# Issuing the four loads of w_in in a different order among GpSimd's casts of v

## The chip, the cores and the metric

The kernel runs on one core of a Trainium2 chip. The metric is device time in microseconds (us) of one execution. Five engines run side by side, each with its own instruction list in a fixed order: PE (TensorE, matrix products), DVE (VectorE), ACT (ScalarE), POOL (GpSimd) and SP (SyncE). DMA transfers are issued by SP, ACT or POOL and are then carried out by the core's 16 DMA engines. An instruction that needs another engine's result waits on a semaphore, and everything behind it on its own engine waits with it.

## What is computed

The reference is sliding-window attention followed by a two-layer network:

```python
# q, k, v: (8 batches, 8 heads, 576 rows, 64)
scores = matmul(q, k^T) / 8;  keep 0 <= row - column < 64, else -1e9
attn   = softmax(scores);     x = matmul(attn, v)      # -> (4608 tokens, 512)
h      = x @ w_in                                       # w_in: (512, 2048)
g      = h / (1 + exp(-1.702 * h))
out    = g @ w_out                                      # w_out: (2048, 512)
```

Inputs and output are float32 in memory. The kernel computes in bf16 with float32 accumulation.

## The kernel before

The 4608 tokens are 36 tiles of 128, and four tiles make a chunk. For each tile the kernel forms the scores (`scores`, L325), the exponentials (`exp`, L340 and L342), the product with v (`pv`, L360), the division (`norm`, L376 and L378) and a transpose of x (`x_mm`, L426). For each chunk it then multiplies by w_in (`up_mm`, L464), applies the activation on ACT (`up_th`, L475) and DVE (`up_g`, L481), and multiplies by w_out (`down`, L494). The order of all instructions on all engines is written out by hand: a call in the source puts its instruction at the end of its engine's list. After L836 slots take over that order; the change touches only the start.

At the start the memory traffic is arranged so:

- **q and k of batch 0, first 512 rows.** SP issues four loads (`load_quads`, L125) and then two loads of v (`load_v(0, 0)`, `load_v(0, 2)`, L87). ACT issues `load_v(0, 1)` and `load_v(0, 3)` (L520, L521). v arrives as float32 in `stage_v`.
- **Casts of v.** `cast_v(b, i, parts=...)` (L101) turns a staged tile of v into bf16. Part 1 is the tile as it is (`v_nat`). Parts 0 and 2 are its two halves moved by 64 rows (`v_off`). `pv` needs both forms. The casts of tile 0 and part 1 of tile 3 are on DVE, the other casts of batch 0's tiles 1 to 3 on POOL. A cast on POOL waits for its tile's load, and what stands behind it on POOL waits too.
- **The weights.** `load_w_in(i)` (L242) is one DMA that POOL issues. It reads a quarter of w_in, casts it to bf16 on the way and writes `w_in_sb[i]`, 512 KB. `load_w_out(j)` (L248) does the same for a quarter of w_out. All eight go into POOL's one queue (q0), which the profile calls software_dynamic. `up_mm` of the first chunk works through w_in quarter by quarter (L580 on, L595 on, L616 on, L628 on).
- **Two gates.** At L522 POOL copies one element out of the last of the first loads, so that no weight is fetched before q and k have come. At L599 POOL copies one element of `w_in_sb[3]` into `stage_qk[0]`. SP's next loads begin with `load_pairs(0, 2)` (L169), which overwrites `stage_qk[0]`, so SP issues nothing from the second v load on until the last quarter of w_in has landed. Behind it SP issues `load_v(0, 4)`, `load_pairs(1, 0)`, two more v loads, and so on.
- **What follows the gate on POOL.** The casts of `load_pairs(0, 2)`, k then q (`cast_pair`, L113, called at L640 and L641), then `load_w_out(2)` and `load_w_out(3)` (L642, L643), then casts of v. On PE, after three groups of `down`, the cast pairs are transposed (`turn_mm`, L196, called at L662 and L663).

Of the kernel before, what the change touches and what calls it, by code (L numbers as in the profile page):

```python
# [29 lines left out]
def kernel(  # L30
# [39 lines left out]
    def size(i):  # L70
        return P if i < 4 else 64

    def heads(ap):
        return ap.rearrange("p (h d) -> p h d", d=D)
# [4 lines left out]
    def stage_of_v(b, i):  # L79
        return stage_v[5 if (b, i) == (0, 4) else i]  # L80
# [10 lines left out]
    def cast_v(b, i, engine=None, parts=(0, 1, 2)):  # L91
        n, vn, vo = size(i), v_nat[b % 2], v_off[b % 2]
        src = heads(stage_of_v(b, i)[:])
        pieces = [
            (vo[64:128, i, :, 0:D], src[0:64]),
            (vn[0:n, i, :, 0:D], src[0:n]),
            (vo[0:64, i + 1, :, 0:D], src[64:128]) if i < 4 else None,
        ]
        for p in parts:
            if pieces[p]:  # L100
                (engine or nc.gpsimd).tensor_copy(out=pieces[p][0], in_=pieces[p][1])  # L101
# [138 lines left out]
    def load_w_in(i):  # L240
        f = slice(512 * i, 512 * i + 512)
        nc.gpsimd.dma_start(  # L242
            out=w_in_sb[i][:], in_=moe_w_in.rearrange("(c p) f -> p c f", p=P)[:, :, f]
        )

    def load_w_out(j):
        f = slice(4 * j, 4 * j + 4)
        nc.gpsimd.dma_start(  # L248
            out=w_out_sb[:, f, :],
            in_=moe_w_out[512 * j : 512 * j + 512, :].rearrange("(p c) d -> p c d", c=4),  # L250
        )
# [269 lines left out]
    load_v(0, 3, nc.scalar)  # L521
    nc.gpsimd.tensor_copy(out=gate[0:1, 0:1], in_=stage_qk[1][0:1, 1, 0:1])  # L522
    load_w_in(0)
    cast_v(0, 1, parts=(0,))
    cast_v(0, 1, parts=(1,))
    cast_v(0, 1, parts=(2,))
    load_w_in(1)
    cast_v(0, 2, parts=(0,))
    cast_v(0, 2, parts=(1,))
    cast_v(0, 2, parts=(2,))  # L530
    cast_v(0, 3, parts=(0,))
    load_w_in(2)
    cast_v(0, 3, parts=(2,))
    load_w_in(3)
    load_w_out(0)
    load_w_out(1)
    cast_quads(0, 0, nc.vector)
# [490 lines left out]
```

## Time and profile before

| | us |
|---|---|
| median of 4 runs | 306.91 (306.19 to 308.47) |
| the profiled execution's own time | 306.75 |
| its span, first to last instruction | 305.0 |
| PE busy | 295.8 (97%) |
| DVE / ACT / POOL busy | 165.4 / 159.2 / 132.8 |
| share of 16 DMA engines: q0 (POOL's) / q1 / q10 (ACT's) | 66.7% / 46.3% / 3.7% |

A profile is one execution. Its time axis starts at the first instruction, and 1.75 us of the execution lie outside the span. In a timeline each line is one instruction or a run of equal ones: start, duration, engine, source line, what it writes and reads, and in square brackets how long the engine had been idle before it and what released it. "x128" is a count. Issue of a DMA and its landing are different things: the issue is an instruction on POOL, SP or ACT, and the landing comes us later, when the last of the 16 DMA engines has written its part. The DMA part of a profile gives bytes moved and the mean busy share of those engines in a stretch.

### The profile page before, as it was taken

What the parts mean: (1) busy time and instruction counts of PE and PEld (TensorE: products, weight loads), DVE (VectorE), ACT (ScalarE), POOL (GpSimd) and SP (SyncE); (2) the same over time, 40 slices, a digit from 0 to 9 for tenths busy, and PEclk for the clock granted to TensorE, in tenths of its full rate; (3) what the DMA queues carried; (4) which work ended last, traced back from release to release, by engine and by line L of the source; (5) the groups of instructions that cost most, each with busy time, mean ns of one, the idle gap of its engine ahead of it and who ended that gap; (6) DMA issues with size and microseconds to landing.
All of it is one profiled execution on the core that took longest, in us unless ns stands there. A gap on an engine that the chain in (4) does not pass through costs nothing.

```text
span 305.0 us, 8195 instructions
## 1 busy us (share of the span) xinstructions
PE 295.8 (97%) x3431; PEld 203.1 (67%) x3431; DVE 165.4 (54%) x286; ACT 159.2 (52%) x261; POOL 132.8 (44%) x191
## 2 busy tenths in 40 slices
PE   7799999999999999999999999999999999999995
PEld 6478454998666777777777777767776554444444
DVE  6467624797416364656647376475574754344300
ACT  3477434876436464755546465455565634444311
POOL 1380263853998679587685538573100000000000
PEclk9799999999999999999999999999999999999999
DMA  6989999998999999999999999999921202100121
GB/s 230 229 134 201 227 208 246 273 174 163 139 169 211 172 125 167 161 120 160 160 182 179 119 133 199 144 178 155 165 58 50 69 2 69 42 29 34 62 77 71
DMA packets 149621, 43.34 MB, mean 142 GB/s; under 512 B 135120, under 2 KB 144592, under 8 KB 149584
## 3 DMA queue, kind: packets, MB, share of 16 engines
q0 software_dynamic: 73008, 13.05, 66.7%
q1 hardware_dynamic: 72768, 26.23, 46.3%
q10 hardware_dynamic: 3808, 3.54, 3.7%
q8 instruction: 27, 0.44, 0.6%
q14 instruction: 10, 0.08, 0.1%
HBM read 36.70 MB, written 9.44 MB: 151 GB/s over the span
## 4 chain that ended last, share of the span: by engine, by line
PE 88%; DMA 6%; issue 3%; POOL 1%; ACT 1%; SPq 0%; DVE 0%; POOLq 0%
PE hps L464 39%; PE ops L494 37%; PE Tacc L360 4%; PE S L325 4%; DMA w_out_sb<-in_moe_w_out_dram 3%; DMA stage_qk<-in_k_dram 3%; PE ops L987 1%; PE S L317 1%; PE pxt L426 1%; SPq L125 0%; PE turn L196 0%; PE pxt L435 0%; POOL rows_q L113 0%; PE idle L515 0%; ACT PT L342 0%
## 5 line engine op out<-in xcount | busy, mean ns | idle before, releaser
L481 DVE SCALAR_TENSOR_TENSOR gT<-th,hps 128x512 bf16<-128x512 bf16 x144 | 98.3, 687 | 94.9 <-ACT th L475 94.9
L494 PE MATMUL ops<-w_out_sb,gT 128*128 128x512 bf16 x560 | 139.1, 379 | 0.3 <-DMA w_out_sb<-in_moe_w_out_dram 0.3
L464 PEld LDWEIGHTS <-w_in_sb 128*128 128x128 bf16 x1440 | 113.9, 113 | 31.0 <-issue 0.5
L475 ACT ACTIVATE th<-hps 128x512 bf16<-128x512 f32 x144 | 85.5, 598 | 87.9 <-PE hps L464 86.1
L494 PEld LDWEIGHTS <-gT 128*128 128x128 bf16 x560 | 52.1, 98 | 47.8 <-issue 0.6
L464 PE MATMUL hps<-xT_dma,w_in_sb 128*128 128x256 bf16 (+1 forms) x512 | 79.7, 299 | 0.0
L464 PE MATMUL hps<-xT_pe,w_in_sb 128*128 128x128 bf16 (+1 forms) x928 | 63.8, 225 | 0.0
L228 POOL COPY v_off<-v_nat 64x528 bf16<-64x528 bf16 x25 | 16.0, 639 | 38.6 <-DMA v_nat<-in_v_dram 36.4
L508 ACT ACTIVATE o_sb<-ops 128x512 f32<-128x512 f32 x33 | 19.8, 601 | 15.8 <-PE ops L494 15.8
L224 POOL DMA_DIRECT2D v_nat<-in_v_dram x25 | 21.5, 859 | 0.0
L223 POOL DMA_DIRECT2D rows_k<-in_k_dram x25 | 21.2, 850 | 0.0
L342 ACT ACTIVATE E<-S 128x1024 bf16<-128x1024 f32 x19 | 19.5, 1028 | 3.2 <-PE S L325 3.0
L223 POOL DMA_DIRECT2D rows_q<-in_q_dram x25 | 21.2, 847 | 0.0
L340 ACT ACTIVATE E<-S 128x512 bf16<-128x512 f32 x26 | 14.1, 594 | 12.6 <-PE S L325 12.6
L347 DVE TENSOR_TENSOR PT<-E,mask_None 128x1024 bf16<-128x1024 bf16 x25 | 17.9, 721 | 1.9 <-ACT E L342 1.7
L101 POOL CAST v_off<-stage_v 64x512 bf16<-64x512 f32 x24 | 15.5, 657 | 7.7 <-DMA stage_v<-in_v_dram 6.7
L403 DVE TENSOR_TENSOR xs<-Tacc,rc 128x896 bf16<-128x896 f32 (+1 forms) x26 | 18.0, 692 | 0.9
L360 PEld LDWEIGHTS <-PT 128*64 128x64 bf16 x576 | 11.0, 110 | 6.7 <-issue 5.9
L360 PE MATMUL Tacc<-v_off,PT 128*64 128x65 bf16 x320 | 13.5, 196 | 0.0
L230 POOL COPY v_off<-v_nat 64x528 bf16<-64x528 bf16 x20 | 12.9, 644 | 1.2
L325 PE MATMUL S<-qt,kt 64*128 64x64 bf16 x576 | 12.6, 192 | 0.0
L325 PEld LDWEIGHTS <-kt 64*128 64x128 bf16 x576 | 9.8, 96 | 4.1 <-issue 3.4
(74 smaller groups left out, 146.3 us busy)
## 6 DMA issues: line engine op xcount, KB each, us to landing
out_dram<-o_sb SPq DMA_DIRECT2D x24, 256.0 KB, 4.4
out_dram<-o_sb ACTq DMA_DIRECT2D x11, 256.0 KB, 2.0
stage_v<-in_v_dram SPq DMA_DIRECT2D x10, 256.0 KB, 5.7
rows_q<-in_q_dram POOLq DMA_DIRECT2D x20, 128.0 KB, 5.3
rows_k<-in_k_dram POOLq DMA_DIRECT2D x20, 128.0 KB, 6.3
v_nat<-in_v_dram POOLq DMA_DIRECT2D x20, 128.0 KB, 6.6
stage_qk<-in_q_dram SPq DMA_DIRECT2D x4, 512.0 KB, 6.7
stage_qk<-in_k_dram SPq DMA_DIRECT2D x4, 512.0 KB, 8.0
```

Of the source, the lines that this page charges most:

```text
L223: nc.gpsimd.dma_start(out=heads(rows[b % 2][w][0:n, i, :]), in_=rows_of(src, b, i))
L224: nc.gpsimd.dma_start(out=v_nat[b % 2][0:n, i, :, 0:D], in_=rows_of(v, b, i))
L325: nc.tensor.matmul(st[h % 2][:, t * 256 + hp * 64 : t * 256 + hp * 64 + 64], lhsT=src[1][part, hp, 64 * j : 64 * j + 128], rhs=src[0][part ...
L342: nc.scalar.activation(out=e[:], in_=st[:], func=AF.Exp, scale=scale)
L347: nc.vector.tensor_tensor(out=pt[:].rearrange("p a f -> p (a f)"), in0=E_of.pop(m)[:].rearrange("p a f -> p (a f)"), in1=masks[z][:].rearr ...
L360: nc.tensor.matmul(out_of(h)[t * 64 : t * 64 + 64, 0 : D + 1], lhsT=pt[:, epos : epos + 64], rhs=win, start=True, stop=True,)
L403: nc.vector.tensor_tensor(out=out[:, :, hs], in0=src[:, :, :, 0:D], in1=rc[:, :, hs].to_broadcast([P, 2, n, D]), op=ALU.mult,)
L464: nc.tensor.matmul(ps[:, g, :], lhsT=w_in[:, c, (f + g) % 4 : 512 : 4], rhs=xT[ch][:, m0 : m0 + nt // P, c, :], start=(c == 0), stop=(c == 3),
L475: nc.scalar.activation(out=th[:], in_=ps[:], func=AF.Tanh, scale=0.851)
L481: nc.vector.scalar_tensor_tensor(out=gT[ch, f // 4][:, f % 4 : f % 4 + nf, t0 : t0 + nt], in0=th[:], scalar=1.0, in1=ps[:], op0=ALU.add, o ...
L494: nc.tensor.matmul(O_of[ch, tsub][:, :], lhsT=gT[ch, j][:, f, tsub * P : (tsub + 1) * P], rhs=w_out_sb[:, 4 * j + f, :], start=(j == 0 and ...
L508: nc.scalar.activation(out=o_sb[:], in_=ps[:], func=AF.Copy, scale=0.5)
```

## The change

```diff
     load_w_in(0)
+    load_w_in(1)
+    load_w_in(2)
     cast_v(0, 1, parts=(0,))
     cast_v(0, 1, parts=(1,))
     cast_v(0, 1, parts=(2,))
-    load_w_in(1)
+    load_w_in(3)
     cast_v(0, 2, parts=(0,))
     cast_v(0, 2, parts=(1,))
     cast_v(0, 2, parts=(2,))
     cast_v(0, 3, parts=(0,))
-    load_w_in(2)
     cast_v(0, 3, parts=(2,))
-    load_w_in(3)
     load_w_out(0)
     load_w_out(1)
```

The lists of PE, DVE, ACT and SP are the same in both programs. On POOL the same instructions stand in another order: quarters 1 and 2 of w_in move ahead of the casts of v's tile 1, quarter 3 takes the place that quarter 1 had, and the remaining casts and the two loads of w_out follow without a load of w_in between them.

## The prediction

> **What bounds the kernel now.** I read the page first: PE is busy 97% of the span, and from slice 3 to the last but one every slice of PE shows 9. So a change at the start pays only as far as it removes PE's idle time. Next I read PE's waits between 20 and 60 us, by whom PE waited for; there are two:
>
> ```profile
> PE turn L196 <- POOL rows_q L113: 1.1, 1, 1.1
> PE ops L494 <- DMA w_out_sb<-in_moe_w_out_dram: 0.3, 1, 0.3
> ```
>
> PE's waits over the whole span add four before 12 us and none after 60 us. So no more than 1.09 + 0.31 = 1.40 us can be won behind the change, all of it before 48 us. Where these waits come from stands in POOL's timeline (start, duration, line, and in brackets the idle time before):
>
> ```profile
> 11.19 0.91 POOL L242 DMA_DIRECT2D w_in_sb<-in_moe_w_in_dram  x1
> 13.88 0.61 POOL L101 CAST v_off<-stage_v 64x512 bf16<-64x512 f32 x1 [1.78 <-DMA stage_v<-in_v_dram]
> ...
> 15.79 0.75 POOL L242 DMA_DIRECT2D w_in_sb<-in_moe_w_in_dram  x1
> ...
> 19.16 0.75 POOL L242 DMA_DIRECT2D w_in_sb<-in_moe_w_in_dram  x1
> ...
> 20.51 0.75 POOL L242 DMA_DIRECT2D w_in_sb<-in_moe_w_in_dram  x1
> 21.25 1.09 POOL L248 DMA_DIRECT2D w_out_sb<-in_moe_w_out_dram  x2
> 28.82 0.18 POOL L599 CAST stage_qk<-w_in_sb 1x1 f32<-1x1 bf16 x1 [6.47 <-DVE gT L481]
> 36.35 1.03 POOL L113 CAST rows_k<-stage_qk 32x1024 bf16<-32x1024 f32 x1 [7.35 <-DMA stage_qk<-in_k_dram]
> 37.33 1.22 POOL L113 CAST rows_q<-stage_qk 32x1024 bf16<-32x1024 f32 x1
> 38.50 1.06 POOL L248 DMA_DIRECT2D w_out_sb<-in_moe_w_out_dram  x2
> ```
>
> The reader is to see a chain. Quarter 3 of w_in, issued at 20.51, takes 8.2 us to land (DMA issues of that stretch), so at 28.7; the gate L599 runs at 28.82 (the DVE result named in its bracket had come at 28.49, and the program's wait on DVE there is for a much earlier one). SP issues `load_pairs(0, 2)` at 29.03. Its k lands at 36.3, POOL casts until 38.55, and PE stands 1.09 us. Behind the casts POOL issues w_out quarters 2 and 3; quarter 3 lands at 47.8 and PE stands 0.31 us. So PE is bound in this stage by the landing of quarter 3 of w_in. It is not bound by w_in itself: from 22.49 us PE runs 128 products on it without a gap, needs quarter 1 at 23.55 (landed 21.7), quarter 2 at 27.9 (24.7) and quarter 3 at 31.4 (28.7).
>
> Last, what the DMA engines do meanwhile, us by us (the last three columns are TensorE's clock, the engines' busy share and GB/s):
>
> ```profile
> 15.00:16.00 1.00, 1.00 (x37) 0.83 (x36) 0.00 (x0) 0.73 (x3) 0.94 (x3) 1.00 1.23 203
> 16.00:17.00 1.00, 1.00 (x28) 0.48 (x22) 0.77 (x2) 0.54 (x2) 0.96 (x2) 1.00 0.22 35
> 17.00:18.00 1.00, 1.00 (x26) 0.79 (x25) 0.34 (x2) 0.95 (x1) 0.87 (x3) 1.00 0.56 77
> ...
> 20.00:21.00 1.00, 1.00 (x29) 0.91 (x28) 0.44 (x1) 0.80 (x3) 1.00 (x2) 1.00 0.99 106
> 21.00:22.00 1.00, 1.00 (x30) 0.96 (x23) 0.70 (x2) 0.89 (x2) 1.00 (x3) 1.00 0.68 99
> ```
>
> Two holes: q0 runs dry at 16.3 and at 20.9, because the next quarter is issued too late (its data start some 1.5 to 2 us after the issue begins: issue 15.79, data 17.24; issue 19.16, data 21.24).
>
> **The change, part by part.** *Two issues move into a wait.* POOL is done with w_in(0) at 12.10 and waits until 13.88 for v's tile 1. Two issues of 0.75 us (row L242) take 1.50 of these 1.78 us; even at the longest row, 0.91, they end at 13.92, 0.04 late. The casts of tile 1 thus stay at 13.88; w_in(3) takes w_in(1)'s place at 15.79 with the same 0.75; the casts of tile 2 and part 0 of tile 3 keep their times. Part 2 of tile 3 comes 0.75 earlier, and the issues of w_out(0) and (1) some 1.45 earlier, at 19.8; they queue behind w_in in q0 in any case. L599 then only waits longer in POOL's list, with nothing behind it that is ready. Nothing is queued behind a new wait; SP, ACT, DVE and PE keep their lists. Cost: nothing, hidden by POOL's wait of 1.78 us. If that cover were gone, the casts would be up to 1.8 us late, against a slack of 1.1 (tile 2 part 1 ends at 17.87, `pv` uses it at 18.99): 0.7 us.
>
> One neighbour changes: DVE's cast of v at 18.63 took 0.87 beside a POOL cast, where its like took 0.43 alone; a second POOL cast now follows the first, so it may lose up to 0.6 more. Its users stand at 20.75 and 21.14, 1.2 us or more after its end, so I take 0 (bound 0.2, through the `norm` behind it).
>
> A rule against the change: the Trainium skill, "SBUF — State Buffer", section "SBUF: two separate sides", says that GpSimd can't write the descriptors of its DMAs while VectorE runs a float32 copy from SBUF to SBUF in a two-port mode. DVE's three casts of v's tile 0 stand at 12.42 to 13.75, just where the two issues go; by the rule these would end some 1.3 us later and PE would lose up to 0.3 us (an estimate). The rows don't show it: the two issues of w_out at 38.50, beside a DVE cast of that kind (38.40 to 38.83), took 1.06 us, and 1.09 at 21.25 without one.
>
> *The holes fill.* Quarters 1, 2 and 3 are now issued by 12.85, 13.60 and 16.54, before q0 needs them. How much earlier does quarter 3 land? From above: all 16 engines gain both holes. At 200 KB per us, 16 to 18 us lacks 400 - 112 = 288 KB (1.4 us) and 20 to 22 lacks 400 - 205 = 195 KB (1.0 us): 2.4 us. From below: the landing is that of the last engine. The completion records of q0 (one 4-byte packet per engine and transfer) give for w_in(0) 15 engines by 16.66 and the last at 17.28, for w_in(3) 15 by 27.43 and the last at 28.35. If it is one engine that lags, it had almost no holes: 17.28 to 17.4 and 20.95 to 21.24, 0.4 us. I see no reason for less than zero. Between 0.4 and 2.4 I go by rows of the last engine: w_in(2), issued to idle engines, took it from 21.24 to 24.32, 3.1 us; w_in(3) 4.0 us (24.32 to 28.35). Three quarters behind 17.28 end at 17.28 + 3 x 3.1 = 26.6 by the first row, and 17.28 + 2 x 3.1 + 4.0 = 27.5 by both: 1.75 and 0.85 earlier than 28.35. I take the middle, 1.3.
>
> The Trainium skill, "DMA: Bandwidth & Descriptors", section "Latency and other measured facts", says that two of the 16 engines are usually slower than the others, probably through GpSimd's descriptor rings. By it the same engine would lag always and the gain would be at the low end, 0.4 to 0.9. In this trace the last 9 packets of w_in(0) run at 79 ns each, the pace of the others, so the lag looks like single delays; that speaks for the middle.
>
> *What follows.* L599, the pairs' issue, their landing, the casts and w_out(2), (3) all move by 1.3. The pairs' data don't start before q0 drains (31.8 in before: q1 moved only 0.06 MB from 28 to 32 us), and q0's end moves by about as much, since w_out(0) and (1) follow w_in without a hole either way. rows_q is then ready at 38.55 - 1.3 = 37.25, before PE asks (37.51): 1.09 us won. PE reaches the last wait 1.09 earlier, at 46.43; w_out(3) lands at 47.79 - 1.3 = 46.5: 0.07 of 0.31 us stays. Sum: 1.09 + 0.24 = 1.3 us. Next in line is w_out(2), which landed at 44.2, 0.1 us before its use; it moves along. After 48 us PE waits for nothing, so the gain stays to the end. 306.75 - 1.3 = 305.45, as a forecast **305.5**; the median of the runs, 306.91, lies 0.16 above the profiled execution. With 0.85 to 1.75, capped at 1.40, this case spans 305.3 to 305.9.
>
> **The rivals.** *A: the lagging engine keeps its time.* For it: 17.28 and 28.35 above. Gain 0 to 0.85, so 305.9 to 306.9. Against it: the even pace of its packets.
>
> *B: more than the records' waits.* PE's ends are modelled, so a busy PE could hide short stalls in 34 to 60 us, such as the four products at 46.48 that took 1.04 instead of 0.86. Ten of these would be worth 1 us: 304.5 to 305.2. Against it: nothing shows what they'd wait for.
>
> *C: slower.* At 13 to 14 us q0 and ACT's v loads share the engines (83 KB and 54 KB in that us). With 1.5 MB instead of 0.5 MB queued, v's tile 1 could land later and hold POOL's casts, and then PE at `pv`, 18.99. The trace prices an early stall: after PE's idle us at 10 to 11 the granted clock is 0.50 from 11.5 to 15, 3.4 us at half speed, 1.7 us of work. It decides once PE stands about as long as then, 1.4 us, so when tile 1 lands after 13.88 + 1.1 + 1.4 = 16.4. Then 1.4 + 1.7 - 1.4 (waits that are covered) = 1.7 us slower: 308.4. Against it: w_in(0) alone keeps q0 full until 16.3, and by then ACT's loads are done (last packet 14.13); what stands behind w_in(0) in the same queue isn't reached.
>
> That the change does nothing at all is the end of A: if quarter 3 lands at 28.7 whatever is queued before it.
>
> **How the numbers follow.** Main case 0.55, A 0.20, B 0.08, C 0.17 (it covers every cost at the start that I don't see). The range reaches from 304.9, with half of B and the 0.3 us by which runs differ, to 307.2, with A whole and the mild part of C; left out are half of B and most of C. Half a per cent, 1.5 us, is about what a measurement can tell here. Against 306.91 the main case's 1.3 us is just below it; I put 0.18 of its 0.55 beyond. Faster: 0.18 + 0.08 = 0.26. Slower: 0.14 of C. Same: 0.60.
>
> **What would show it.** In the profile after: POOL's first cast of v still at 13.9; no hole in the DMA rows from 16 to 22 us; L599 at 27.5 instead of 28.82 and SP's issue right behind it; PE's wait for rows_q gone, and that for w_out under 0.1 us. Wrong would be: L599 within 0.4 us of 28.82 (A); a wait of PE at `pv` or a low clock after 15 us (C); the waits gone, but the span not shorter by their sum.

## The result, and the profile after

The median went from 306.97 us (55 runs, 305.1 to 312.32) to 304.68 us (34 runs, 303.38 to 306.55): ratio 0.9929, 95% interval 0.9914 to 0.9945, so 1.7 to 2.6 us faster (2.2 us in the middle). Forecast were 1.3 us, with 305.5 as the time and 304.9 to 307.2 as the range. Executions whose time lay over 1.5% above the fastest of their kernel are left out of every ratio below. The profiled execution of the kernel after took 304.01 us (span 302.3 us), that of the kernel before 306.75 us (305.0 us).

POOL's timeline of the kernel after (start, duration, line, count, and in brackets the idle time before):

```profile
10.51 2.41 POOL L242 DMA_DIRECT2D w_in_sb<-in_moe_w_in_dram  x3
13.55 0.61 POOL L101 CAST v_off<-stage_v 64x512 bf16<-64x512 f32 x1 [0.64 <-DMA stage_v<-in_v_dram]
...
15.46 0.75 POOL L242 DMA_DIRECT2D w_in_sb<-in_moe_w_in_dram  x1
...
19.58 1.08 POOL L248 DMA_DIRECT2D w_out_sb<-in_moe_w_out_dram  x2
25.25 0.18 POOL L599 CAST stage_qk<-w_in_sb 1x1 f32<-1x1 bf16 x1 [4.59 <-DVE gT L481]
31.87 1.03 POOL L113 CAST rows_k<-stage_qk 32x1024 bf16<-32x1024 f32 x1 [6.45 <-DMA stage_qk<-in_k_dram]
32.86 1.03 POOL L113 CAST rows_q<-stage_qk 32x1024 bf16<-32x1024 f32 x1
33.84 1.06 POOL L248 DMA_DIRECT2D w_out_sb<-in_moe_w_out_dram  x2
```

The three issues take 2.41 us and the first cast still waits 0.64 us for its tile: POOL's wait did hide the two issues. The gate L599 runs at 25.25 instead of 28.82, which is 3.57 us earlier, not 1.3. Of that 0.68 us is not the change's: the first gate L522 started 0.68 us earlier in this execution, because the first loads landed earlier. The change's share is 2.9 us.

The stretches that showed the two holes (last three columns: granted clock, the DMA engines' share, GB/s):

```profile
16.00:17.00 1.00, 0.90 (x19) 0.48 (x18) 1.00 (x2) 0.51 (x2) 0.89 (x3) 1.00 1.22 203
17.00:18.00 1.00, 0.45 (x16) 0.33 (x15) 0.14 (x1) 0.94 (x1) 0.94 (x2) 1.00 1.25 208
20.00:21.00 1.00, 1.00 (x22) 1.00 (x19) 0.96 (x3) 0.69 (x2) 0.66 (x2) 1.00 1.24 211
21.00:22.00 1.00, 1.00 (x22) 1.00 (x20) 0.71 (x2) 0.89 (x2) 0.00 (x0) 1.00 1.25 204
```

35, 77, 106 and 99 GB/s became 203 to 211: both holes are full. PE at the two places, first in the kernel before, then in the kernel after:

```profile
34.76 2.75 PE L494 MATMUL ops<-w_out_sb,gT 128*128 128x512 bf16 x12
38.61 0.36 PE L196 MATMUL turn<-ident,rows_q 32*128 32x32 bf16 x8 [1.09 <-POOL rows_q L113]
...
46.48 1.04 PE L494 MATMUL ops<-w_out_sb,gT 128*128 128x512 bf16 x4
47.83 1.89 PE L494 MATMUL ops<-w_out_sb,gT 128*128 128x512 bf16 x8 [0.31 <-DMA w_out_sb<-in_moe_w_out_dram]
49.65 0.41 PE L325 MATMUL S<-qt,kt 64*128 64x64 bf16 x16
```

```profile
33.41 2.75 PE L494 MATMUL ops<-w_out_sb,gT 128*128 128x512 bf16 x12
36.09 0.36 PE L196 MATMUL turn<-ident,rows_q 32*128 32x32 bf16 x8
...
43.97 2.76 PE L494 MATMUL ops<-w_out_sb,gT 128*128 128x512 bf16 x12
46.66 0.41 PE L325 MATMUL S<-qt,kt 64*128 64x64 bf16 x16
```

L196 has no bracket any more, and the twelve products at 43.97 run unbroken. Between 20 and 60 us PE waits for nothing.

The brackets show less than a wait costs. A bracket counts from the end of the product before it, but in an unbroken row the next product starts before that end: twelve products at 33.41 take 2.75 us, and L196 starts 2.68 us behind their start. In the kernel before it starts 3.85 us behind it, so this wait cost 1.17 us, not 1.09. From the start of the row at 46.48 to L325 it was 3.17 us, and is 2.69 now: w_out had cost 0.48 us, not 0.31. By PE's starts the two waits cost 1.65 us, not 1.40.

So the change did what it says, and the two waits are gone. In these two executions PE is 2.99 us ahead at L325 (46.66 against 49.65): some 1.65 us are the two waits, and 1.36 us had been won by PE's first product of `up_mm`, which starts at 18.41 instead of 19.77. That second part is no work of the change: the execution before had a PE wait of 1.47 us at 10 us and then half clock until 15 us, and the execution after had a wait of 0.70 us there and full clock. The executions differ by only 306.75 - 304.01 = 2.74 us, because the kernel after loses 0.3 us again near 143 us (at the end of the experiments). But two executions are no medians, and the medians say 2.2 us, more than the 1.40 us that the prediction called the most that could be won. The experiments ask where the rest comes from.

### The profile page after: what moved, and what is told of

Same layout as the page of the kernel before. It is cut to its first block, busy times and chain, and to the rows that moved or that the text cites. A ratio compares the mean times of both kernels' runs of the same rounds, so it can differ in the third digit from the quotient of the medians.

```text
span 302.3 us, 8195 instructions
## 1 busy us (share of the span) xinstructions
PE 295.2 (98%) x3431; PEld 203.5 (67%) x3431; DVE 166.2 (55%) x286; ACT 159.0 (53%) x261; POOL 133.4 (44%) x191
## 4 chain that ended last, share of the span: by engine, by line
PE 90%; DMA 6%; POOL 1%; DVE 1%; SPq 0%; issue 0%; ACT 0%; POOLq 0%
PE hps L464 41%; PE ops L494 39%; PE Tacc L360 4%; PE S L325 3%; DMA xT_dma<-xs 2%; DMA stage_v<-in_v_dram 2%; DMA stage_qk<-in_k_dram 2%; PE ops L987 1%; PE turn L196 1%; PE pxt L426 1%; POOL v_off L101 1%; DVE xs L403 0%; PE pxt L435 0%; POOL v_nat L101 0%; POOL w_in_sb L242 0%
## 5 line engine op out<-in xcount | busy, mean ns | idle before, releaser
L494 PE MATMUL ops<-w_out_sb,gT 128*128 128x512 bf16 x560 | 139.0, 379 | 0.0
L494 PEld LDWEIGHTS <-gT 128*128 128x128 bf16 x560 | 52.2, 98 | 47.3
L360 PE MATMUL Tacc<-v_nat,PT 128*64 128x65 bf16 x256 | 12.3, 196 | 0.6 <-POOL v_nat L101 0.6
L325 PE MATMUL S<-qt,kt 64*128 64x64 bf16 x576 | 12.4, 191 | 0.0
```

The lines of the kernel that those rows point to most:

```text
L325: nc.tensor.matmul(st[h % 2][:, t * 256 + hp * 64 : t * 256 + hp * 64 + 64], lhsT=src[1][part, hp, 64 * j : 64 * j + 128], rhs=src[0][part ...
L360: nc.tensor.matmul(out_of(h)[t * 64 : t * 64 + 64, 0 : D + 1], lhsT=pt[:, epos : epos + 64], rhs=win, start=True, stop=True,)
L494: nc.tensor.matmul(O_of[ch, tsub][:, :], lhsT=gT[ch, j][:, f, tsub * P : (tsub + 1) * P], rhs=w_out_sb[:, 4 * j + f, :], start=(j == 0 and ...
```

## The experiments

The first theory was that the start's half clock had hidden something: at full clock PE comes earlier and waits longer behind it ("cover", theory 1). The second was that the clock itself is the extra gain, so that executions at full clock are faster. The prediction's own account was that nothing after 48 us matters. Against it, another idea came up on the way: a second place, near 93 us, where PE's `scores` (L325) need `kt`, which SP transposes (L235) at the end of the long stream that starts at the gate L599. The expectations number further theories, each explained where it stands.

**b_again: the kernel before, unchanged.** No edit.

> The kernel before once more, unchanged, to see how often TensorE's clock is halved for 3.4 us near the start, and what that costs. Theory 1 (cover): in the kernel before, PE waits near 37 us for the cast of rows_q, whose time is set by the landing of w_in quarter 3; a PE that comes 1.3 us earlier because its clock was not halved only waits 1.3 us longer. So executions at a mean clock of 0.999 or more and those near 0.994 take the same time within 0.4 us, about 306.9, and a profile at full clock shows a wait of about 2.4 us at L196. Theory 2 (the clock is the extra gain): executions at full clock take about 305.5 and those at 0.994 about 306.9; the change is worth 1.3 us in either.

306.94 us, ratio 1.0018 [0.9992, 1.0043]. Its profiled execution took 305.90 us with clock 0.999 and had these waits of PE between 20 and 60 us (total, times, longest):

```profile
PE turn L196 <- POOL rows_q L113: 1.2, 1, 1.2
PE ops L494 <- DMA w_out_sb<-in_moe_w_out_dram: 0.4, 1, 0.4
```

1.60 us instead of 1.40 by the brackets, so cover is real but small: 2.4 us at L196 had been expected, 1.2 came. As an account of the whole gain it falls: in four groups of runs of before, those whose mean clock lay under 0.9965 had medians of 307.1 to 308.2 us, and those above it 306.06 to 306.55. Cover had asked for equal times, the second theory for 305.5 against 306.9, and neither holds. Note also that the profiled execution was the fastest of its 11 at full clock, 0.96 us under their median (306.86). A profile of this kernel can show fewer waits than a typical execution has.

**a_gate_late: the kernel after, with the late gate put back.** L599 waits for the second w_out load in place of the last w_in load.

```diff
-    nc.gpsimd.tensor_copy(out=stage_qk[0][0:1, 0, 0:1], in_=w_in_sb[3][0:1, 0, 0:1])
+    nc.gpsimd.tensor_copy(out=stage_qk[0][0:1, 0, 0:1], in_=w_out_sb[0:1, 4, 0:1])
```

> The changed kernel, but the gate L599 reads quarter 1 of w_out, which lands some 5 us after quarter 3 of w_in. Theory 1: the gain comes through the gate, so L599 runs near 30 us instead of 25.3, the cast of rows_q ends near 37, PE waits about 1 us at L196 and some more for w_out quarter 3; 305.5 to 306.5 us, most of the gain gone. Theory 3 (the gain comes from w_in, w_out or the casts of v themselves, not through the gate): 304.7, as the changed kernel.

307.29 us, ratio 1.0005 [0.9972, 1.0039]: the whole gain is gone, so it does come through the gate. L599 ran at 30.24, but q0 had drained by then, the pairs landed fast and `rows_q` was ready at 35.48. PE's two waits, which theory 1 wanted back, are gone here as well. This is PE near 93 us in that kernel:

```profile
93.39 0.53 PE L325 MATMUL S<-qt,kt 64*128 64x64 bf16 x24
95.31 0.29 PE L325 MATMUL S<-qt,kt 64*128 64x64 bf16 x8 [1.40 <-DMA kt<-rows_k]
```

PE arrives early, does 24 of 32 products, and stands 1.40 us for `kt`; at 77.7 us it had already stood 0.42 us for an earlier `kt`. Counted by PE's starts against those in a_again (below), the two cost 2.2 us, as much as the change had won. Removing the two waits pays nothing when the stream behind the gate doesn't come earlier too. No theory had this; it is where the second place came from.

**b_gate_early: the kernel before, with the gate on quarter 2.** `w_in_sb[3]` at L599 becomes `w_in_sb[2]`.

> The kernel before, but the gate L599 reads quarter 2 of w_in, which landed at 24.7 us, so it opens some 4 us earlier while q0 still has its holes and drains at 31.8 to 34.6 us as before. If the load of the pairs has to wait for q0 to drain, as the prediction had it: L599 at 24.8, the pairs' landing not more than 0.5 us earlier, 306.5 to 306.9 us. If the time of the gate itself counts (theory 1 in its simple form): the pairs land by 32 us, no wait at L196, 304.5 to 305.2 us.

306.48 us, ratio 1.0013 [0.998, 1.0045]. L599 ran at 24.67, earlier even than in the kernel after, but SP's loads got little of the DMA engines while q0 still had w_in and w_out to move: from 25 to 31 us q1 moved 0.06 MB and q0 1.22 MB. `rows_k` was cast at 34.14, 2.2 us earlier than in the kernel before, where at most 0.5 had been expected. The two waits shrank to 0.2 and 0.6 us in its profile, which was the fastest of its runs (304.85), but the median didn't move. So an early gate alone wins nothing: the pairs' k landed 0.8 us behind the last of the six loads queued in q0 (34.09 and 33.25), as it landed 1.3 us behind it in the kernel before (36.29 and 34.98) and 1.6 in the kernel after (31.82 and 30.25). What counts is q0's end, which the filled holes bring forward.

**a_cold: the kernel after without the two `warm(6)`** at L544 and L548, dummy products that keep PE busy.

> The changed kernel without the 12 filler products (two warm(6), which compute nothing that is used) that stand before and behind the cast of half 1 of q, so that PE idles longer near 9 us and its clock is halved in all or most executions. Theory 1: nothing covers PE's delay any more, so the time is 305.0 to 305.6, 0.7 to 1.3 us over the changed kernel at full clock, and the mean clock 0.994 or less. If the time stays at 304.4 with a clock of 0.994, the lost speed is covered in the changed kernel too, and theory 1 fails.

305.17 us, ratio 0.9957 [0.9934, 0.9981]. Six of 12 runs had a mean clock of 0.992 to 0.994; their median was 305.35 us, that of the others 305.10. Half clock at the start costs little here, and the test doesn't tell the first two theories apart, because the runs at full clock became slower too. Part of the cover lies earlier than theory 1 had it: at full clock PE waits 0.56 us at `pv` near 17 us (b_again, a_again, after), and a late PE doesn't (before, a_cold).

**a_again: the kernel after, unchanged**, on the chip of the three that follow. No edit.

> The changed kernel once more, unchanged, on the chip that also runs the next three and the kernel before, for a comparison on one chip and a second profile. Expected: 1.9 to 2.3 us under the kernel before, L599 near 25, no wait of PE at L196 or for w_out.

304.31 us, ratio 0.9944 [0.9918, 0.9969]: 1.7 us (0.9 to 2.5) under the kernel before, a little less than the 1.9 to 2.3 expected. L599 at 25.55, and no wait at L196 or for w_out.

**hole1_only and hole2_only: one hole filled.** The order on POOL (w: load of a w_in quarter, v: casts of a tile):

```
before      w0 | v1 | w1 | v2 v30 | w2 | v32 | w3
hole1_only  w0 w1 | v1 | v2 v30 | w2 | v32 | w3
hole2_only  w0 | v1 | w1 w2 | v2 v30 v32 | w3
after       w0 w1 w2 | v1 | w3 | v2 v30 v32
```

> The kernel before with quarter 1 alone moved ahead of the casts of v's tile 1; quarters 2 and 3 stay where they were. Theory 1 (what counts is when the last weights of q0 have come, and every quarter that is issued too late leaves a hole): quarter 1 ends 1 us earlier, but quarter 2 is still issued near 19, so the hole at 17 only moves to 19 to 21; L599 and q0's end as before within 0.4 us, time within 0.4 us of the kernel before. Theory 4 (issuing quarter 1 early is what helps, because PE uses it first): 304.5 to 305.5 us.

> The kernel before with quarter 2 alone moved up, right behind quarter 1 (so both stand behind the casts of v's tile 1). Theory 1: the hole at 17 us stays, that at 21 goes; L599 1.0 to 1.5 us earlier than in the kernel before, PE's waits at L196 and for w_out about 1 us shorter in sum: 0.7 to 1.2 us under the kernel before, about half of the change's gain.

hole1_only: 306.34 us, ratio 1.0006 [0.9977, 1.0035]. Nothing: the hole only moves behind quarter 1, and L599 stays at 28.33, with both waits of PE:

```profile
PE turn L196 <- POOL rows_q L113: 1.4, 1, 1.4
PE ops L494 <- DMA w_out_sb<-in_moe_w_out_dram: 0.4, 1, 0.4
```

hole2_only: 305.38 us, ratio 0.9967 [0.9936, 0.9998]. L599 at 26.67, both waits gone, and about 0.9 us (0.1 to 2.0), some half of the gain. Its PE waits between 20 and 110 us:

```profile
PE S L325 <- DMA kt<-rows_k: 0.3, 1, 0.3
```

Again PE runs into `kt`. With the gate 1.7 us earlier than in b_again, the two waits (1.6 to 1.8 us) are gone but not the limit behind them; with the gate 2.8 us earlier (a_again) both are. The order of hole2_only has a cost of its own, though: quarter 2's issue now stands ahead of the casts of tile 2 too, PE waits 1.48 us at `pv` near 17 us instead of 0.56, and its first product of `up_mm` starts at 19.09 instead of 18.43 (b_again). A later PE also meets fewer waits. So the two holes don't add up as shares: in these orders the second alone is worth half, the first alone nothing.

**w3_last and w3_last_2: a version that goes further.** Quarter 3 is issued behind all casts.

```diff
     load_w_in(2)
     cast_v(0, 1, parts=(0,))
...
-    load_w_in(3)
...
     cast_v(0, 3, parts=(2,))
+    load_w_in(3)
     load_w_out(0)
```

> The changed kernel with quarter 3 issued behind all of POOL's casts of v's tiles 1 to 3 instead of behind the first three. In the changed kernel at full clock PE waits 0.6 us at pv of tile 2 for part 1 of v's tile 2, which stands 0.75 us behind because of that issue. Theory 1: the issue is at about 18.8, its data could start by 20.8, and q0 needs them at 20.5 to 21, so no hole or one under 0.4 us; the wait at pv is gone: 0.3 to 0.6 us under the changed kernel. If instead a hole of a us opens before quarter 3, there are still 2 us to spare until PE needs rows_q, so the time doesn't rise.

> The kernel with quarter 3 behind all casts once more: 0.5 to 1.0 us under the changed kernel (304.3 to 304.7), so 303.4 to 304.0 us, and 2.3 to 3.2 us under the kernel before of the same call.

303.3 us, ratio 0.9913 [0.9872, 0.9955], and 303.55 us, ratio 0.9904 [0.9874, 0.9934]. On the same chip the median was 1.0 us under a_again, where 0.3 to 0.6 had been expected; the executions of the two overlap (302.88 to 306.87 and 303.58 to 305.28). It takes away a wait that the kernel after has at full clock, 0.56 us by its bracket for `v_nat` at 17.6 (`pv`), since the casts of tile 2 come one issue earlier; by PE's starts that wins 0.8 us. q0 has three quarters queued meanwhile, and L599 stays at 25.1 to 25.7. In w3_last_2 PE then waits 0.56 us for w_out again.

**b_look2 and b_look3: one execution each of the kernel before.**

> The kernel before, unchanged, for a further profile of PE's waits. The prediction took the 1.40 us of waits (L196 and w_out) of one profiled execution as the most that can be won. Theory 5 (that execution's waits were small): the waits differ from one execution to the next, and 1.5 to 2.5 us is usual at full clock. If they are 1.40 or less here too, the extra gain comes from elsewhere.

> As the run before it, one more profile of the kernel before: 1.5 to 2.5 us of waits at L196 and for w_out by theory 5, 1.40 or less otherwise.

311.32 and 312.29 us; single executions give no ratio. Their waits at L196 and for w_out were 0.6 and 1.5 us in sum; theory 5, by which 1.5 to 2.5 us is usual, isn't borne out by these. The first also waited 0.80 us for w_in itself near 22 us, which the prediction had ruled out from one execution. Both stood at `kt`, 2.80 and 4.19 us; the first:

```profile
98.19 0.29 PE L325 MATMUL S<-qt,kt 64*128 64x64 bf16 x8 [2.80 <-DMA kt<-rows_k]
```

**a_more_dma: the kernel after with four more transfers** of 128 KB on POOL, ahead of `pe = {}`.

```diff
+    for i in range(2):
+        for w in range(2):
+            nc.gpsimd.dma_start(out=rows[i][w][:, 5, :], in_=moe_w_in[0:P, 0:DM])
     pe = {}
```

> The changed kernel with four more DMAs of 128 KB each (a corner of w_in, cast to bf16, into rows that nothing reads any more), issued by POOL near 78 us: 2.5 us of the 16 engines' time at q0's pace of 200 KB per us, and 3.4 us of POOL. Theory 6 (the DMA engines, busy 99% until 220 us, bound the kernel, and what the change won is the 2.4 us of holes): 1 to 2.5 us slower than the changed kernel, with new waits of PE for kt or xT. Theory 5 (the gain is the waits near 37 and 46 us, and behind them the transfers have time to spare): within 0.5 us of the changed kernel.

310.91 us, ratio 1.0146 [1.0102, 1.0189], some 6 us over the kernel after, far beyond both theories. PE stood 4.78 us at `kt` (97.50), and the mean clock of all six runs was 0.989 to 0.994, so 3.7 to 6.8 us of 309 at half clock. But the edit adds two things, 512 KB and some 3.4 us of POOL's time.

**a_pool_copies: five copies more on POOL at the same place, and no transfer.**

```diff
+    for i in range(5):
+        nc.gpsimd.tensor_copy(out=rows[0][0][:, 5, :], in_=w_in_sb[0][:, 0, 0:512])
     pe = {}
```

> The kernel after with five copies of 128x512 bf16 more on POOL ahead of the slots, some 0.6 us each, 3 us in all, and no DMA more. If the 3.4 us of POOL's issues made the run with four more transfers slow, kt lands some 3 us later here too, PE waits 1.5 to 3 us at the scores near 93 us, the clock is halved behind that, and the time is 307 to 310 us. If the 512 KB on the DMA engines did it, POOL's own slack (1.3 and 0.5 us of waits near 91 and 95 us) takes up most of it and the time is 304.3 to 305.3 us.

310.94 us, ratio 1.0153 [1.0114, 1.0192]: the same again, and a little over the 307 to 310 us of the first branch. The five copies, POOL's timeline:

```profile
75.01 3.31 POOL L840 COPY rows_q<-w_in_sb 128x512 bf16<-128x512 bf16 x5
```

The issue of `kt` and its time to landing (a DMA view over that issue), and PE:

```profile
kt<-rows_k SPq DMA_TRANSPOSE x1, 6.6
```

```profile
92.34 0.52 PE L325 MATMUL S<-qt,kt 64*128 64x64 bf16 x24
97.11 0.39 PE L325 MATMUL S<-qt,kt 64*128 64x64 bf16 x8 [4.25 <-DMA kt<-rows_k]
```

And the clock behind that wait (clock, DMA share, GB/s at the end of each line):

```profile
95.00:96.00 1.00, 0.00 (x0) 0.00 (x0) 0.00 (x0) 0.00 (x0) 0.00 (x0) 1.00 0.09 10
96.00:97.00 1.00, 0.00 (x0) 0.00 (x0) 0.00 (x0) 0.00 (x0) 0.07 (x1) 0.67 1.57 254
...
98.00:99.00 1.00, 1.00 (x4) 0.30 (x2) 0.40 (x1) 0.57 (x1) 1.00 (x2) 0.50 1.89 223
...
102.00:103.00 1.00, 1.00 (x4) 0.34 (x3) 0.39 (x1) 0.99 (x2) 0.31 (x1) 0.50 1.91 194
103.00:104.00 1.00, 1.00 (x15) 0.82 (x14) 0.00 (x0) 0.00 (x0) 0.94 (x3) 0.91 2.38 156
```

SP issues `kt` at 90.46, 4.0 us later than in a_again (86.44), and it lands 6.6 us behind its issue instead of 4.8. So POOL's time alone is enough: from 69.4 us on POOL works without a wait until `kt` is issued (from 69.1 in a_again), and 3.3 us more there are 4.25 us of PE's wait and half clock from 96.4 to 103.2 us, some 6 us of it behind the wait. This place is a bound in waiting, with a slack of 1.0 to 1.4 us in the kernel after.

**b_no_store and a_no_store: both kernels without the four stores of chunk 0**, so the first 512 rows of the output stay unwritten. The test `if ch > 0:` stands ahead of the store at L510.

> The kernel before without the four stores of chunk 0 (the first 512 rows of the output stay unwritten), so that SP's stream between 49 and 57 us has four transfers less and kt lands earlier near 93 us. Theory 'second place' (kt and PE meet near 93 us): kt lands 1 us or more ahead of PE there, the waits at L196 and w_out stay (about 1.1 to 1.8 us together), and the time is 0.3 to 0.7 us under the kernel before (305.5 to 306.0), with no execution in the slower tail. Theory 'first place only' (all gain lies in the waits near 37 and 46 us): the time is that of the kernel before within 0.2 us.

> The kernel after without the four stores of chunk 0 (the first 512 rows of the output stay unwritten). Theory 'second place': kt is no limit in the kernel after, so this takes as long as the kernel after, 304.2 to 304.5 us, and the difference to the kernel before without these stores is 1.3 to 1.8 us, what the waits near 37 and 46 us alone are worth. Theory 'first place only': the difference between the two kernels without stores is the whole 2.0 to 2.2 us.

305.89 us, ratio 0.9982 [0.9959, 1.0005], and 303.97 us, ratio 0.9911 [0.9887, 0.9936]. The kernel before without stores fell into the range of "second place", and none of its 12 executions was over 307.88, but the interval of its ratio includes no change. The gap between the two kernels is 1.92 us, between the 1.3 to 1.8 of the one theory and the 2.0 to 2.2 of the other, so the pair doesn't decide. It also missed its aim: `kt` came only 0.5 us ahead of PE in b_no_store, not 1, and in a_no_store PE even waited for it:

```profile
93.25 0.29 PE L325 MATMUL S<-qt,kt 64*128 64x64 bf16 x8 [0.33 <-DMA kt<-rows_k]
```

**The second place in one table.** `kt` lands: the landing of its DMA in the trace. PE needs it: for the last eight of 32 products, of which the first starts 0.36 us behind the run's start in an unbroken run (nine executions alike). Where PE waits, its bracket is some 0.1 us shorter than the missing slack, as it counts from the end of the 24th product.

| profiled execution | L599 | kt lands | PE needs it | slack, us | brackets at L196 and w_out |
|---|---|---|---|---|---|
| before | 28.82 | 95.61 | 95.78 | 0.2 | 1.40 |
| b_again | 28.36 | 94.89 | 94.64 | -0.2 | 1.60 |
| hole1_only | 28.33 | 93.49 | 93.90 | 0.4 | 1.8 |
| hole2_only | 26.67 | 93.95 | 93.48 | -0.5 (bracket 0.35) | 0 |
| a_gate_late | 30.24 | 95.27 | 93.75 | -1.5 (bracket 1.40) | 0 |
| a_pool_copies | 25.03 | 97.06 | 92.70 | -4.4 (bracket 4.25) | 0 |
| after | 25.25 | 91.84 | 92.80 | 1.0 | 0 |
| a_again | 25.55 | 91.28 | 92.73 | 1.4 | 0 |

The gate's time alone doesn't set `kt`; the rest of the stream varies from one execution to the next. In b_again the run of 32 products is 0.94 us long instead of 0.64, without a bracket: 0.30 us of waiting inside a busy row. The kernel before has its two early waits and, behind them, little slack (-0.2 to 0.4 us); PE just meets `kt` because it was already held up. The change moves `kt` by 3.8 us and PE by 3.0 us, and so makes slack.

**A third place, near 143 us.** The kernel after meets one more limit, which no theory named: `up_mm` needs `xT_dma`, a transpose that SP issues (L448). PE in a_again, then in b_again:

```profile
142.16 1.03 PE L494 MATMUL ops<-w_out_sb,gT 128*128 128x512 bf16 x4
143.81 1.91 PE L464 MATMUL hps<-xT_dma,w_in_sb 128*128 128x256 bf16 x16 [0.62 <-DVE gT L481]
```

```profile
144.37 1.03 PE L494 MATMUL ops<-w_out_sb,gT 128*128 128x512 bf16 x4
145.24 1.91 PE L464 MATMUL hps<-xT_dma,w_in_sb 128*128 128x256 bf16 x16
```

The bracket names DVE, but the transpose decides: in a_again it landed at 143.67, and in all seven executions with this wait the product starts 0.13 to 0.14 us behind that landing. By PE's starts a_again loses 0.78 us here, the profiled execution of the kernel after 0.32, b_no_store and a_gate_late have brackets of 0.62 and 0.57, and before, b_again, hole1_only and a_no_store lose nothing. Behind 150 us PE's starts run parallel to the end in all profiles, so what an execution gains or loses is decided at these places.

## Why the prediction was right and wrong

- *What is removed and moved on POOL*: right. The issues fitted into the wait (2.41 us, 0.64 us of wait left), nothing was late behind them, L196's wait went and w_out's wait went. The slack of 1.1 us that the prediction gave the casts of tile 2 held for its half-clocked execution alone: at full clock PE waits 0.56 us for one of them, before the change (b_again) as after it.
- *The cost to DVE's casts*: the casts of v's tile 0 beside the issues took 0.68 and 0.72 us instead of 0.42 and 0.43, and POOL's issues 0.80 us each, within the 0.75 to 0.91 us of before. The rule of the Trainium skill, "SBUF — State Buffer", section "SBUF: two separate sides", was read as POOL having to wait; here, if anything, the casts did, which the same section allows: it gives the port that the two engines share to whichever starts first. Nothing stood behind them on PE in this profile; that the two are linked is an inference from their places.
- *How much earlier quarter 3 lands*: mis-sized, 1.3 us forecast and 2.9 us measured, over the upper bound of 2.4. The bound counted four of the rows; over all twelve from 16 to 28 us the engines of the kernel before moved 1871 KB, and at the 206 KB per us of the kernel after that is 2.9 us short of full. For the estimate below the bound, the lag of the last engine was read as a slower engine with its own holes. With the holes filled, its completion in q0 comes 1.5 to 1.6 us behind the eighth engine's for the first four w_in and two w_out loads alike (17.18 against 15.59, 24.80 against 23.32, 29.82 against 28.24), and the last one takes 2.54 us from one quarter to the next, where the prediction had put 3.1 and 4.0. It is a constant delay, not a slower pace, so the last engine gains the holes whole. This speaks against the use that the prediction made of the Trainium skill, "DMA: Bandwidth & Descriptors", section "Latency and other measured facts" (two engines usually slower): with an engine slower in pace the gain would have been 0.4 to 0.9 us. That one completion comes late each time, the trace does show; it doesn't name the engine.
- *The step that failed*: "no more than 1.40 us can be won behind the change", with "after 48 us PE waits for nothing, so the gain stays to the end". The cap was a sum of brackets in one execution. By PE's starts the same two waits cost 1.65 us there, 1.84 in b_again and 2.0 in hole1_only. And the view of waits didn't show that `kt` near 95 us came 0.2 us ahead of need: a limit with no wait to its name, at which b_again lost 0.30 us more. a_gate_late shows what it is worth: with the two waits gone and the stream not earlier, the gain is nothing. Together with the mis-sized landing this is, as far as the profiles show, why 2.2 us were won and not 1.3.
- *Had the landing come out as forecast*, a gain of about 1 us would have been near: hole2_only has the gate 1.7 us earlier than b_again and gains about 0.9 us, with a later PE as its own cost. The larger move made the larger gain, through a place that the prediction didn't know.
- *Rival B* (more than the records' waits, chance 0.08) was the nearest, and its ground was right: PE's ends are modelled, and that hides part of a wait, 0.25 us of the two here. Its example was not a stall, though: four products of L494 take 1.03 to 1.04 us in unbroken rows too. And the stall that no bracket shows at all was at 94 us, not in 34 to 60.
- *Rival A* fell with the constant delay, and *rival C* with the first cast at 13.55 and full clock behind 15 us.
- *What stays open*: at 100 us b_again is 2.2 us behind a_again by PE's starts: 0.1 from the start, 1.26 at L196, 0.58 for w_out, 0.30 at `kt`. That is the gain that the medians show. The two executions differ by only 305.90 - 304.38 = 1.52 us, since a_again then loses 0.78 at the third place. So one pair accounts for the gain by places; it is a pair from two chips, and its own times differ by less than the medians of the main comparison. How often a typical execution of either kernel loses time at `kt` or at `xT_dma` is not shown: b_again's profiled execution lay 1.0 us under its median, and the pair without stores didn't settle it.

## What to carry to other kernels

A list of waits shows what PE waited for, not what it nearly waited for, and its brackets show less than a wait costs: take the distance between starts, and compare it with an unbroken row. Before capping a gain at the waits, follow the same stream to its next users and take landing minus need, for a stall taken out of PE makes everything behind it due that much sooner. Ask of every moved transfer what else hangs on it; here one gate starts the whole stream of loads, so moving it was worth more than the two waits behind it. Where runs spread by 1% and the gain is less, compare two or three executions' waits, since the profiled one may be the fastest of its kind.

## What the runs showed of the hardware

- The length of one PE wait doesn't tell whether the clock is halved. A wait of 1.47 us at 10 us (kernel before) came just before 3.4 us at clock 0.50 (11.5 to 15.0), and one of 1.20 us at 9.5 us (a_cold) likewise. One of 1.65 us at 8.3 us (w3_last) was not followed by it, nor one of 1.40 us at 94 us (a_gate_late, where the clock stayed at 1.00 through 104 us). During one of 4.25 us (a_pool_copies) the clock fell to 0.50, for 6.8 us.
- Transfers issued on SP while POOL's queue was full made nearly no way: 0.06 MB in 6 us against 1.22 MB (b_gate_early).
- A run of 32 products lengthened from 0.64 to 0.94 us without being shown as a wait (b_again, L325): a short stall can hide in a busy row.
- In an unbroken row products of L494 start every 0.22 us and each is 0.38 us long in the record, so a wait's bracket is up to 0.17 us shorter than its cost (0.31 against 0.48 us for w_out in the kernel before).
